# A fused linear-attention and gated-MLP kernel: 24 normalizations on ScalarE, 52 low parts on GpSimd, a new order of all steps

## The chip, the core and the metric

The kernel runs on one core of a Trainium2 chip. The core's engines work side by side, each through its own queue in order: TensorE (PE, with its weight loads as PEld), VectorE (DVE), ScalarE (ACT), GpSimd (POOL) and SyncE (SP), which here only issues DMAs. Semaphores tie the queues together. The metric is the device time of one execution in microseconds, as the median of several runs.

## What is computed

For 8 batches of 576 tokens, 8 heads of 64 (512 channels), float32 throughout:

```python
kv  = einsum('bhsd,bhse->bhde', k, v); out = einsum('bhsd,bhde->bhse', q, kv)
x   = out / sqrt(mean(out*out, -1) + 1e-6) * g_norm        # then heads side by side: [b, 576, 512]
h   = gelu_tanh(x @ w_in); u, v = h[..., :512], h[..., 512:]
v_n = (v - mean(v)) / sqrt(var(v) + 1e-6) * g_ln           # per token
v_s = einsum('ts,bsd->btd', w_sg, v_n) + b_sg[None, :, None]
y   = x + (u * v_s) @ w_out
```

## The kernel before

Every float32 operand of the large matrix products is split into a high part, rounded to the matmul type, and a low part, the rest; each product is then three matmuls (high·high, high·low, low·high). The split costs, per operand tile, one cast and one subtraction on another engine.

The whole program is one hand-recorded list of steps, `ORDER`, with one name per step: a letter for the kind, a digit for the batch, a number for the tile, and for some kinds a last letter that names the engine (v DVE, a ACT, p POOL). Each engine executes its own steps in the order in which they stand in that list, so the list alone sets every queue, SP's too. `HOMES` is a second list that says which buffer each new tile takes.

The kinds that matter here, with their lines: `k` loads of k and v (L405) and `q` loads (L431); `K` k^T v (pkv, L414); `o` attention output (pq, po, L439), `e` its squares (L451), `f` its scaling (L459 on ACT, L461 on DVE); `s` sums of squares (pss, L484) and `t` the reciprocal roots (L514 to L528); `x` scaling to x (L568), `X` and `Y` its high and low parts (L230, L584); `U` and `u` the product and gelu of u (pu L666, L671); `V` and `a` the product and gelu of v (pv L615, L620), four chunks of 128 tokens a batch and one leftover chunk for two batches; `b` the statistics of v (L625, L626), `p` its reciprocal deviation on POOL (L630, L631), `y` its normalization on DVE (L636), `z` and `w` its high part (L230) and low part (L653); `S` the product over tokens (pg, L680, L683), `g` its scale and bias (L688), `G` the gate u·v_s on POOL (L693); `H` and `J` the high and low part of a gate, `R` a difference of two gates (L721), `h` and `W` its high and low part (L230, L709 for both kinds of low part); `P` the output product (py, L741), `Q` and `Z` its addition to x (L754); `O` the store. `N` is a matmul on zeros ("warm") that only fills time at the start. The output product uses seven block products of sums and differences instead of eight blocks, so `P72` is the third product of batch 7.

In steady state the batches overlap: TensorE's queue mixes `U` and `V` of one batch with `S` of the one before and `P` of the one before that, so that each step's operands are made while TensorE does something else. One casting helper (L230) serves all high parts.

Of the kernel before, what the change touches and what calls it, by code (L numbers as in the profile page):

```python
# [835 lines left out]
```

## Time and profile before

| | us |
|---|---|
| timed runs: median (lowest to highest of 3) | 496.63 (494.15 to 496.92) |
| the profiled execution's own time | 491.86 |
| its span, first to last instruction | 490.1 |
| TensorE matmuls busy | 482.1 (98%) |
| DVE busy | 351.3 (72%) |
| ACT busy | 179.8 (37%) |
| POOL busy | 159.1 (32%) |

Shares are averages over the span. TensorE's busy share counts overlapped matmuls and says little alone; what counts is whether its queue ever waits, stretch by stretch. An idle engine that nobody waits for costs nothing.

### The profile page before, as it was taken

What the parts mean: (1) busy time and instruction counts of PE and PEld (TensorE: products, weight loads), DVE (VectorE), ACT (ScalarE), POOL (GpSimd) and SP (SyncE); (2) the same over time, 40 slices, a digit from 0 to 9 for tenths busy, and PEclk for the clock granted to TensorE, in tenths of its full rate; (3) what the DMA queues carried; (4) which work ended last, traced back from release to release, by engine and by line L of the source; (5) the groups of instructions that cost most, each with busy time, mean ns of one, the idle gap of its engine ahead of it and who ended that gap; (6) DMA issues with size and microseconds to landing.
All of it is one profiled execution on the core that took longest, in us unless ns stands there. A gap on an engine that the chain in (4) does not pass through costs nothing.

```text
span 490.1 us, 10060 instructions
## 1 busy us (share of the span) xinstructions
PE 482.1 (98%) x3989; PEld 440.8 (90%) x3989; DVE 351.3 (72%) x809; ACT 179.8 (37%) x442; POOL 159.1 (32%) x204
## 2 busy tenths in 40 slices
PE   6999999999999999999999999999999999999997
PEld 6668889998998999988998998998998899998997
DVE  1698698888777786468765875577767687577576
ACT  1668575155234331142223323335033332123220
POOL 0333142652232323332143113342305232442551
PEclk9999999999999999999999999999999999999999
DMA  8996793054343612064535443300331021100033
GB/s 228 361 353 232 220 277 104 2 157 141 104 142 89 142 43 74 1 192 130 175 75 185 117 104 117 100 1 1 97 104 49 1 62 43 49 1 0 2 122 120
DMA packets 33658, 55.36 MB, mean 113 GB/s; under 512 B 7308, under 2 KB 9228, under 8 KB 33612
## 3 DMA queue, kind: packets, MB, share of 16 engines
q1 hardware_dynamic: 33612, 54.73, 37.1%
q8 instruction: 31, 0.51, 0.4%
q14 instruction: 15, 0.12, 0.1%
HBM read 44.76 MB, written 9.95 MB: 112 GB/s over the span
## 4 chain that ended last, share of the span: by engine, by line
PE 96%; DMA 2%; DVE 0%; ACT 0%; SPq 0%; issue 0%
PE pu L666 21%; PE pg L680 21%; PE pv L615 20%; PE py L741 18%; PE pkv L414 5%; PE pg L683 3%; PE po L439 3%; PE pss L484 2%; DMA kv_first<-in_vx 1%; DMA kv_first<-in_kx 1%; PE psq L468 1%; PE pq L439 1%; PE pb L552 1%; PE warm L270 0%; SPq L405 0%
## 5 line engine op out<-in xcount | busy, mean ns | idle before, releaser
L693 POOL TENSOR_TENSOR u<-gt,u 128x288 f32<-128x288 f32 x64 | 56.3, 890 | 116.3 <-DVE gt L688 113.6
L680 PE MATMUL pg<-wsh,vh 128*128 128x288 f32 x256 | 75.8, 296 | 0.0
L680 PE MATMUL pg<-wso,vh 128*128 128x288 f32 x256 | 75.4, 294 | 0.0
L680 PE MATMUL pg<-wsh,vo 128*128 128x288 f32 x256 | 75.4, 294 | 0.0
L754 DVE SCALAR_TENSOR_TENSOR x<-py,x 128x288 f32<-128x288 f32 x112 | 49.4, 451 | 28.7 <-PE py L741 28.3
L709 DVE TENSOR_TENSOR g<-u,g 128x288 fp32r<-128x288 f32 x112 | 56.2, 517 | 15.7 <-ACT g L230 13.0
L688 DVE SCALAR_TENSOR_TENSOR gt<-pg,glt,b_bc 128x288 f32<-128x288 f32 x64 | 32.3, 512 | 35.2 <-PE pg L683 34.9
L741 PE MATMUL py<-g,woh 128*128 128x288 f32 x256 | 55.9, 295 | 0.0
L230 ACT CAST g<-u 128x288 fp32r<-128x288 f32 x75 | 30.8, 434 | 68.2 <-POOL u L693 52.3
L671 ACT ACTIVATE u<-pu 128x288 f32<-128x288 f32 x64 | 25.7, 411 | 68.3 <-PE pu L666 67.1
L680 PEld LDWEIGHTS pg<-wsh,vh 128*128 128x128 f32 x256 | 48.2, 188 | 0.8 <-DVE gt L688 0.4
L680 PEld LDWEIGHTS pg<-wso,vh 128*128 128x128 f32 x256 | 48.1, 188 | 0.1
L680 PEld LDWEIGHTS pg<-wsh,vo 128*128 128x128 f32 x256 | 48.1, 188 | 0.0
L666 PE MATMUL pu<-xh,wuh 128*128 128x288 f32 x256 | 45.5, 299 | 0.0
L721 POOL TENSOR_TENSOR u<-u 128x288 f32<-128x288 f32 x33 | 29.4, 894 | 49.6 <-DVE g L709 40.9
L666 PE MATMUL pu<-xo,wuh 128*128 128x288 f32 x256 | 44.3, 295 | 0.0
L666 PE MATMUL pu<-xh,wuo 128*128 128x288 f32 x256 | 44.3, 295 | 0.0
L620 ACT ACTIVATE hv<-pv 128x512 f32<-128x512 f32 x32 | 19.0, 598 | 66.5 <-PE pv L615 59.5
L741 PEld LDWEIGHTS py<-g,woh 128*128 128x128 f32 x256 | 42.7, 188 | 0.6 <-issue 0.4
L741 PE MATMUL py<-g,wxh 128*128 128x288 f32 x192 | 41.5, 295 | 0.0
L666 PEld LDWEIGHTS pu<-xh,wuh 128*128 128x128 f32 x256 | 37.6, 188 | 3.7 <-issue 1.9
L741 PE MATMUL py<-g,woo 128*128 128x288 f32 x128 | 37.8, 295 | 0.0
(123 smaller groups left out, 1005.6 us busy)
## 6 DMA issues: line engine op xcount, KB each, us to landing
q<-in_qT SPq DMA_DIRECT2D x32, 288.0 KB, 5.5
out_y<-x SPq DMA_DIRECT2D x28, 288.0 KB, 2.9
bc<-rd SPq DMA_DIRECT2D x28, 256.0 KB, 3.9
k<-in_kx SPq DMA_DIRECT2D x24, 256.0 KB, 4.9
v<-in_vx SPq DMA_DIRECT2D x24, 256.0 KB, 4.8
kv_first<-in_kx SPq DMA_DIRECT2D x8, 256.0 KB, 6.3
kv_first<-in_vx SPq DMA_DIRECT2D x8, 256.0 KB, 5.4
words<-in_wu SPq DMA_DIRECT2D x4, 512.0 KB, 8.4
```

What stands on the lines that cost most here:

```text
L230: e.copy(dst, src) if e is ac else e.tensor_copy(dst, src)
L414: nc.tensor.matmul(part["kv", b][64 * r : 64 * r + 64, n * 64 : n * 64 + 64], k_[b, c][:, h], v_[b, c][:, h], start=(c == 0 and n == 0), s ...
L615: nc.tensor.matmul(pv, a[cc], w[:, cc, :], start=(n == 0), stop=(n == 11))
L666: nc.tensor.matmul(pu[:, :HS], w[:, cc, f], a[b, cc][:, t], start=(i == 0), stop=(i == 11))
L671: ac.activation(u_[b, n], part["u", b, n][:, :HS], AF.Gelu_apprx_tanh, scale=W_UP)
L680: nc.tensor.matmul(ps[:, :HS], a[:, d], w[:, c, t], start=(i == 0), stop=False)
L688: ve.scalar_tensor_tensor(g_[b, n], ps[:, :HS], glt[:, dc : dc + 1], b_bc[:, half(n // 4)], op0=ALU.mult, op1=ALU.add)
L693: po.tensor_tensor(u_[b, n], g_[b, n], u_[b, n], op=ALU.mult)
L709: ve.tensor_tensor(lo, src, f32(hi), op=ALU.subtract)
L721: e.tensor_tensor(dst, x, y, op=ALU.subtract)
L741: nc.tensor.matmul(y_[b, bank][c][:, :HS], wo_block(h, blk, e)[:, block(c)], a, start=(start and i == 0), stop=(i == 5), skip_group_check= ...
L754: ve.scalar_tensor_tensor(xs, y_[b, bank][c][:, :HS], W_UP, xs, op0=ALU.mult, op1=ALU.add)
```

## The change

Three things change. (1) `y` gets an engine: 24 of the 36 normalizations go from one DVE instruction to three ACT instructions (negate the mean, multiply by the reciprocal deviation, then one activation with a scale and a bias per partition). (2) The low parts `J`, `W` and `w` get an engine: 16 of 48 `J`, 26 of 64 `W` and 10 of 36 `w` go from DVE to POOL, the others stay on DVE. (3) `ORDER` and `HOMES` are replaced throughout. With it a few dozen further steps change engine (for instance `H` on ACT 39 instead of 31, `R` on POOL 29 instead of 33, `x` on POOL 4 instead of 8, low parts of weights on POOL 4 instead of 1), and 71 `N` instead of 69 stand in the list. The number of all other TensorE steps is the same.

```diff
@@ HOMES and ORDER: every row differs; a few of ORDER's
-    k01 k02 k04 D21 F21 D23 D02 A02 E02 B02v L02 C02 F02v I02v k00 N899 N898 N897 N896 N895 N894 N893 N892 N891 N890
-    W64 y70 R66p h66v R62v h63a u74 V72 H63v a71 W63 Q60 b71 h65a W65 z70a w70 W66 a72 Z56 b72 p71 V73 y71 U75 a73 b73
-    z71a w71 p72 p73 u72 P63 U76 Z60 y72 P62 Q63 z72a y73 u76 h62v z73a H67v J67 J63 R67p u75 w72 w73 J66 S71 g71 G71
...
+    k02 D23 D22 k04 D21 F21 k01 D00 A00 k00 N899 N898 N897 N896 N895 N894 N893 N892 N891 N890 N889 N888 N887 N886 N885
...
+    z52v R42v V53 w50v Q40 P41 G47 k73 Z40 Q41 a53 o61 b53 e63 Z41 e61 h44v W44v e67 f67v e65 w52p R43p K71 c70v s60
+    t60 U53 t61 t62 f65a f63a h43a W43v p53 y53a z53a t63 t64 t65 t66 q72 w53v f61a t67 t68 R45v U52 u53 w51p S53 g53
...
+    R63p V70 h62a a70 b70 h60v W60v h61a V71 a71 b71 p70 y70v V72 a72 W61v R65v z70a u70 p71 J66v R64v w70v V73 U73
+    b72 p72 O57 y71v a73 b73 u74 h63a P63 U77 P60 y72v h64v H63a W64v p73 y73v z71a z72a z73a w72v W63v H67a w71v J67v
+    w73v Q60 h65v W65p W62v u77 S77 g77 Z63 Z60 J63v u73 S71 g71 G71 R67v H71v P62 S75 g75 Q63 Q62 O56 S70 G77 Z62
@@ -631,8 +633,14 @@
         po.tensor_tensor(rs, rs, mhalf, op=ALU.pow)
         st_[b, c] = st_[b, c], rs
 
-    def v_norm(b, c):
+    def v_norm(b, c, e):
         mv, rs = st_[b, c]
+        if e is ac:
+            shift = T([P, 1], F32, "nb")
+            ac.mul(shift, mv[:, 0:1], -1.0)
+            ac.mul(shift, shift, rs[:, 0:1])
+            ac.activation(hv_[b, c], hv_[b, c], AF.Identity, bias=shift[:, 0:1], scale=rs[:, 0:1])
+            return
         ve.tensor_scalar(hv_[b, c], hv_[b, c], mv[:, 0:1], rs[:, 0:1], op0=ALU.subtract, op1=ALU.mult)
 
     def v_high(b, c, e):
@@ -647,10 +655,10 @@
                 part["vl", r] = T([P, F], F32R, "vl%d" % r)
                 cast(e, part["vl", r][s], hv_[b, c][s])
 
-    def v_low(b, c):
+    def v_low(b, c, e):
         if c < NC:
             hi, lo = vn_[b, c]
-            ve.tensor_tensor(lo, hv_[b, c], f32(hi), op=ALU.subtract)
+            e.tensor_tensor(lo, hv_[b, c], f32(hi), op=ALU.subtract)
         else:
             for r in range(2):
                 s, o = last_rows(r)
@@ -704,15 +712,15 @@
         gs_[b, key] = [T([P, HS], F32R, "h", 28, nm="g") for _ in range(2)]
         cast(e, gs_[b, key][0], src)
 
-    def split_low(b, key, src):
+    def split_low(b, key, src, e):
         hi, lo = gs_[b, key]
-        ve.tensor_tensor(lo, src, f32(hi), op=ALU.subtract)
+        e.tensor_tensor(lo, src, f32(hi), op=ALU.subtract)
 
     def gate_high(b, n, e):
         split_high(b, operand(n), u_[b, n], e)
 
-    def gate_low(b, n):
-        split_low(b, operand(n), u_[b, n])
+    def gate_low(b, n, e):
+        split_low(b, operand(n), u_[b, n], e)
 
     def combine(b, n, e):
 
@@ -726,8 +734,8 @@
     def combined_high(b, n, e):
         split_high(b, combined(n), combined_tile(b, n), e)
 
-    def combined_low(b, n):
-        split_low(b, combined(n), combined_tile(b, n))
+    def combined_low(b, n, e):
+        split_low(b, combined(n), combined_tile(b, n), e)
 
     def y(b, n):
         blk, op, bank, start, _ = PRODUCTS[n]

```

What the list moves is shown at three places, one engine each.

**SP's queue at the start.** The first loads of k and v (kv_first, the leftover rows k and v), constants (gnt, glt, ext) and weight words. Before:

```order
L405 DMA kv_first_77<-in_kx 128x512
L405 DMA kv_first_78<-in_vx 128x512
L405 DMA kv_first_77<-in_kx 128x512
L405 DMA kv_first_78<-in_vx 128x512
L405 DMA k_92<-in_kl 64x512
L405 DMA v_93<-in_vl 64x512
L295 DMA gnt_65<-in_gn 128x1
L300 DMA glt_67<-in_gl 128x4
L287 DMA words_100<-in_wu 128x2x512
L405 DMA kv_first_77<-in_kx 128x512
L405 DMA kv_first_78<-in_vx 128x512
```

Now:

```order
L407 DMA kv_first_77<-in_kx 128x512
L407 DMA kv_first_78<-in_vx 128x512
L302 DMA glt_67<-in_gl 128x4
L300 DMA ext_91<-in_ex 64x512
L407 DMA k_93<-in_kl 64x512
L407 DMA v_94<-in_vl 64x512
L297 DMA gnt_65<-in_gn 128x1
L407 DMA kv_first_77<-in_kx 128x512
L407 DMA kv_first_78<-in_vx 128x512
L289 DMA words_102<-in_wu 128x2x512
L407 DMA kv_first_77<-in_kx 128x512
L407 DMA kv_first_78<-in_vx 128x512
```

The constant `ext` (64x512) and `glt` stand ahead of the second pair of kv_first; the third pair, which was issues 10 and 11, is now 11 and 12.

**ACT's queue at the last v of batch 5,** from its gelu (hv<-pv) to its high part (vh). `sq` and `x<-po` belong to the attention of batch 6, `g` are casts of gates. Before:

```order
L620 ACTIVATE hv_4481<-pv_4459 128x512
L230 CAST g_4483<-u_3977 128x288
L230 CAST g_4486<-u_3866 128x288
L451 ACTIVATE sq_4517<-po_4505 128x288
L451 ACTIVATE sq_4519<-po_4508 128x288
L459 ACTIVATE x_4327<-po_4508,g8_66 128x288
L451 ACTIVATE sq_4547<-po_4511 128x288
L451 ACTIVATE sq_4549<-po_4514 128x288
L459 ACTIVATE x_4415<-po_4505,g8_66 128x288
L230 CAST vh_4600<-hv_4417 128x512
L230 CAST vh_4600<-hv_4481 128x512
```

Now:

```order
L622 ACTIVATE hv_4593<-pv_4557 128x512
L453 ACTIVATE sq_4611<-po_4598 128x288
L453 ACTIVATE sq_4614<-po_4595 128x288
L453 ACTIVATE sq_4620<-po_4604 128x288
L453 ACTIVATE sq_4623<-po_4601 128x288
L461 ACTIVATE x_4191<-po_4601,g8_66 128x288
L461 ACTIVATE x_4372<-po_4598,g8_66 128x288
L232 CAST g_4683<-u_3680 128x288
L640 ACTIVATE nb_4690<-mv_4608 128x1
L641 ACTIVATE nb_4690<-nb_4690,rs_4687 128x1
L642 ACTIVATE hv_4593<-hv_4593,nb_4690,rs_4687 128x512
L232 CAST vh_4553<-hv_4593 128x512
```

Between the gelu and the cast there are now the three instructions of the normalization (nb, nb, hv); one cast of a gate (g) and the high part of an earlier v chunk (vh) left the stretch. In the new list TensorE's steps between that v (`V53`) and the first product that reads it (`S53`) are `P41`, `o61`, `K71`, `s60`, `U53` and `U52`.

**DVE's queue at the last v of batch 7,** from its statistics to the low part that the next product needs. Before:

```order
L626 BN_AGGR mv_5903<-st_5902 128x2
L653 TENSOR_TENSOR vo_5859<-hv_5846,vh_5858 128x512
L754 SCALAR_TENSOR_TENSOR x_4327<-py_5713,x_4327 128x288
L636 TENSOR_SCALAR hv_5863<-hv_5863,mv_5867,rs_5908 128x512
L754 SCALAR_TENSOR_TENSOR x_4477<-py_5916,x_4477 128x288
L636 TENSOR_SCALAR hv_5900<-hv_5900,mv_5903,rs_5911 128x512
L230 CAST g_5964<-u_5353 128x288
L230 CAST g_5968<-u_5530 128x288
L709 TENSOR_TENSOR g_5969<-u_5530,g_5968 128x288
L709 TENSOR_TENSOR g_5844<-u_5304,g_5843 128x288
L653 TENSOR_TENSOR vo_5959<-hv_5863,vh_5958 128x512
L653 TENSOR_TENSOR vo_5959<-hv_5900,vh_5958 128x512
```

Now:

```order
L627 BN_STATS st_5920<-hv_5918 128x6
L628 BN_AGGR mv_5921<-st_5920 128x2
L644 TENSOR_SCALAR hv_5868<-hv_5868,mv_5910,rs_5913 128x512
L232 CAST g_5971<-u_5474 128x288
L717 TENSOR_TENSOR g_5972<-u_5474,g_5971 128x288
L644 TENSOR_SCALAR hv_5918<-hv_5918,mv_5921,rs_5978 128x512
L661 TENSOR_TENSOR vo_5984<-hv_5868,vh_5983 128x512
L717 TENSOR_TENSOR g_5927<-u_5433,g_5926 128x288
L661 TENSOR_TENSOR vo_5873<-hv_5845,vh_5872 128x512
L717 TENSOR_TENSOR g_5990<-u_5202,g_5989 128x288
L661 TENSOR_TENSOR vo_5984<-hv_5918,vh_5983 128x512
```

Two additions to x (x<-py) and one cast left the stretch, one low part (g<-u,g) joined it; the normalizations here stay on DVE. Between the last v and the first pg TensorE has four steps before (`U`, `P`, `U`, `P`) and four now (`U73`, `P63`, `U77`, `P60`).

## Rows read from the trace of the kernel before

**Rows 1.** The page's head: span, and busy time (share of the span) and instructions of TensorE's matmuls and weight loads, DVE, ACT and POOL.

```profile
span 490.1 us, 10060 instructions
PE 482.1 (98%) x3989; PEld 440.8 (90%) x3989; DVE 351.3 (72%) x809; ACT 179.8 (37%) x442; POOL 159.1 (32%) x204
```

**Rows 2.** Busy time by stretch: from:to in us, its length, then busy us (instructions) of PE, PEld, DVE, ACT and POOL, the granted TensorE clock, the mean busy share of the DMA engines, GB/s.

```profile
0.00:12.38 12.38, 8.31 (x46) 8.12 (x47) 1.67 (x11) 2.15 (x3) 0.19 (x4) 1.00 0.84 228
12.38:34.50 22.12, 21.45 (x263) 13.91 (x263) 17.49 (x40) 13.64 (x33) 6.81 (x6) 1.00 1.04 355
...
38.80:90.00 51.20, 51.20 (x373) 46.64 (x372) 43.39 (x98) 34.44 (x83) 17.03 (x22) 1.00 0.61 185
...
390.00:486.90 96.90, 96.85 (x687) 94.10 (x685) 70.17 (x159) 24.32 (x59) 37.47 (x45) 1.00 0.14 47
486.90:490.10 3.20, 0.00 (x0) 0.00 (x0) 0.45 (x1) 0.00 (x0) 0.00 (x0) 0.81 0.33 116
```

**Rows 3.** The chain of waits at the start, in order of time: start us, us, what.

```profile
6.80 5.46 DMA kv_first<-in_vx
...
12.39 2.87 PE pkv L414 x80
15.26 1.50 PE warm L270 x11
...
33.42 1.20 PE po L439 x16
...
37.54 1.34 PE pss L484 x31
38.88 6.57 PE pu L666 x48
...
51.98 1.23 PE pkv L414 x32
```

**Rows 4.** Groups of matmuls by line: operation, tiles, shapes, count, busy us, mean ns of one, and idle us of the engine before them.

```profile
L680 PE MATMUL pg<-wsh,vo 128*128 128x288 f32 x256 | 75.4, 294 | 0.0
L666 PE MATMUL pu<-xh,wuo 128*128 128x288 f32 x256 | 44.3, 295 | 0.0
```

**Rows 5.** The same view for the instructions that the change moves and their neighbours, on DVE, POOL and ACT.

```profile
L636 DVE TENSOR_SCALAR hv<-hv,mv,rs 128x512 f32<-128x512 f32 x32 | 18.4, 582 | 1.9 <-POOL rs L631 1.8
L653 DVE TENSOR_TENSOR vo<-hv,vh 128x512 fp32r<-128x512 f32 x32 | 22.0, 698 | 5.0 <-ACT vh L230 4.9
L709 DVE TENSOR_TENSOR g<-u,g 128x288 fp32r<-128x288 f32 x112 | 56.2, 517 | 15.7 <-ACT g L230 13.0 <-PE py L741 1.9
L754 DVE SCALAR_TENSOR_TENSOR x<-py,x 128x288 f32<-128x288 f32 x112 | 49.4, 451 | 28.7 <-PE py L741 28.3
L230 DVE CAST g<-u 128x288 fp32r<-128x288 f32 x37 | 12.5, 352 | 2.6 <-POOL u L721 1.8 <-POOL u L693 0.7
L721 POOL TENSOR_TENSOR u<-u 128x288 f32<-128x288 f32 x33 | 29.4, 894 | 49.6 <-DVE g L709 40.9 <-DVE u L721 8.2
L568 POOL TENSOR_TENSOR x<-x,bc 128x512 f32<-128x512 f32 x8 | 11.9, 1494 | 17.1 <-DMA bc<-rd 6.4 <-ACT xlh L595 5.3 <-DVE xlo L600 5.3
L631 POOL TENSOR_TENSOR rs<-rs,mhalf 128x1 f32<-128x1 f32 x36 | 23.0, 640 | 3.0
L620 ACT ACTIVATE hv<-pv 128x512 f32<-128x512 f32 x32 | 19.0, 598 | 66.5 <-PE pv L615 59.5 <-issue 5.5 <-DVE vo L653 1.5
L451 ACT ACTIVATE sq<-po 128x288 f32<-128x288 f32 x56 | 20.7, 414 | 16.3 <-PE po L439 15.7 <-PE py L741 0.3
L459 ACT ACTIVATE x<-po,g 128x288 f32<-128x288 f32 x41 | 20.1, 505 | 3.1 <-DMA out_y<-x 3.0
L230 ACT CAST vh<-hv 128x512 fp32r<-128x512 f32 x25 | 15.3, 621 | 6.9 <-DVE hv L636 6.9
L230 ACT CAST g<-u 128x288 fp32r<-128x288 f32 x75 | 30.8, 434 | 68.2 <-POOL u L693 52.3 <-POOL u L721 9.9 <-DVE u L721 3.9
L260 ACT ACTIVATE g<-eps 128x1 f32<-128x1 f32 x1 | 0.2, 202 | 0.0
L671 ACT ACT_TABLE_LOAD x1 | 1.3, 1283 | 0.0
```

**Rows 6.** Timeline of batch 7 between its last v and the first pg: start us, us, engine, line, operation, count.

```profile
448.00 0.69 PE L666 MATMUL pu<-xh,wuh 128*128 128x288 f32 x4
...
448.83 0.69 DVE L625 BATCH_NORM_STATS2 st<-hv 128x6 f32<-128x512 f32 x1 [1.40 <-ACT hv L620]
...
453.27 1.90 DVE L653 TENSOR_TENSOR vo<-hv,vh 128x512 fp32r<-128x512 f32 x2
...
453.43 1.19 POOL L721 TENSOR_TENSOR u<-u 128x288 f32<-128x288 f32 x1 [2.25 <-DVE g L709]
...
455.43 0.29 PE L680 MATMUL pg<-wsh,vo 128*128 128x288 f32 x1
```

**Rows 7.** Timeline of SP's DMA issues at the start: start us, us of the issue, what.

```profile
5.40 0.47 SPq L405 DMA_DIRECT2D kv_first<-in_kx  x1
6.80 0.33 SPq L405 DMA_DIRECT2D kv_first<-in_vx  x1
...
15.90 0.47 SPq L298 DMA_DIRECT2D ext<-in_ex  x1
```

**Rows 8.** The chain of waits in the middle: two blocks of 12 matmuls, the first right behind a block of small pkv matmuls.

```profile
109.92 1.79 PE pu L666 x12
...
113.31 1.59 PE pu L666 x12
```

More of the change, by code (lines that the diff above doesn't have):

```diff
@@ L166 @@
-    f60a a52 b52 p52 R44v R41v z50a z51a g43 G43 H43a h41v R46v y52 Z40 J43 W41 U55 V53 w51 G47 R43p Q40 O36 f64a u55
-    a53 h43a h42a P41 Q41 Z41 o61 e61 e63 f63a R45v b53 W43 K71 w50 c70v e65 e67 s60 t60 t61 p53 y53 t62 t63 h46v f61a
-    t64 H46v U54 z52a U56 z53a t65 t66 t67 w52 f65a t68 r60 u54 P43 W42 R47p w53 J46 h45v W45 Q43 u56 S50 g50 W46 r62
-    f67a S55 g55 G55 S56 g56 S54 h44a W44 Z43 G50 H47v J47 x61p P42 Q42 r61 x60v P45 Q45 U53 l63 U57 u57 g54 Z42 G54
-    H50a l61 q72 S51 l60 Z45 U52 X61a u53 P44 J50 Q44 h47a Y61v l62 r63 x62v S52 Z44 m6 X62a S53 n63 G56 O45 u52 x63v
@@ new lines @@
+    s13 t10 t11 t12 t13 t14 C06 t15 u02 F04a F05a U06 K20 t16 t17 I05v t18 U04 f16a D20 F20a F06a n03 I06v D16 D07
+    F16a I21v f17a A07 E07 D08 f11a B07a L07 C07 k23 A08 f15a D09 U05 u05 I20v A09 B09v r10 I04v F07a B08a I07v k24
+    D10 A10 n00 B10a u06 n01 n02 U07 K21 D14 V02 a02 A14 B14a E09 V01 L09 E08 D18 F18a u04 L08 E10 r12 x10v c20a L10
+    C08 F08v x11v r11 l12 l11 V00 a01 l13 l10 k30 b01 V03 m1 n10 I18v C10 b02 n11 X11a Y11v n12 n13 V04 k31 F10a X10a
+    a00 b00 E14 r13 p02 k32 x12v x13v y02a C09 L14 Y10v p00 K30 u07 X12a p01 X13a Y13v q31 Y12v V10 y00a C14 a04 b04
@@ new lines @@
+    D12 A12 z00a I10v y01a D15 D11 A11 F14v z01a w00v q21 B12v I16v p04 y04a D17 E12 L12 C12 I08v I14v B11v U15 u15
+    U11 u11 a03 b03 p03 F17a I17v U14 u14 z02a w02v d00v A15 z04a B15v D13 A13 D19 F19a F30v d01v a10 y03a U16 U12
+    I30v d02v E15 E13 k33 B13v L13 z03a w01v w03v u16 C13 V11 w04v I19v F32a V13 a13 k40 E11 L11 D24 q20 S02 g02 G02
+    F31a S06 a11 b11 d03v F33a p11 I31v S01 I32v S03 L15 H02v C15 F15a g01 G01 b10 S07 k34 I15v F09a I09v y11a b13
+    d04p F34a S05 C11 u12 p10 g07 d05v J02v G07 S04 H01a I33v g05 g03 G03 y10a F35a S00 d06v g06 z10a z11a G05 U10
@@ new lines @@
+    I34p g00 u10 J01v K31 k42 q22 g04 G00 H00a J00v p13 F11a R01v o20 P00 Q00 R03v H03a w10v G04 R00v I11v d07p h01a
+    e22 W01v e26 f26a c30a J03v I35v H07v f22a q30 V12 Z00 P01 Q01 Z01 h00a W00v U13 G06 R04p F36a P03 R05v y13a e20
+    f20a e24 f24v F37a I37p a12 U17 b12 p12 h05a h04a u13 H06a k41 q23 J06p w11p W05v I36v u17 y12a o21 W04v P02 J07v
+    e27 z12a z13a w13p Q03 Z03 P05 Q02 Q05 w12v e23 e21 e25 s20 t20 t21 f23a t22 t23 t24 t25 t26 t27 S12 t28 r20 f27a
+    r22 S17 g17 r21 R06v h06a R02v h02v W02v f25a h03a S11 g11 S10 Z02 W03p P04 Z05 R07p h07a g10 W07p G10 G11 H11a
@@ new lines @@
+    W06v g12 Z04 S14 Q04 g14 P06 G14 Z06 Q06 G12 f21v x20v S13 x21v g13 O05 H12a H10v J11v l21 S16 l20 X21a q32 J10v
+    S15 X20a g15 Y21v P10 l23 l22 m2 o30 e34 e32 Y20v f32a r23 K40 x22v x23v k51 g16 G16 X22a Y22v X23a e36 O06 G15
+    f34a Y23v V20 a20 O04 q33 e30 R11p R10p V22 a22 b22 U20 u20 f30a b20 U21 u21 k44 G17 k43 G13 O07 f36v o31 e31 e33
+    R13v n22 K41 e35 e37 s30 f37v t30 U26 J12v t31 t32 t33 h11a t34 t35 h10a f33a U24 n23 t36 t37 t38 R12p W10p R14v
+    q43 p22 y22v u26 U27 U22 u24 h12v W12p f31a V21 H16a h14a W14v u22 k50 J16v h13a c40a W11v a21 U23 n21 u23 q52
@@ new lines @@
+    f43a S34 g34 G34 Q26 r42 x41v x40v S37 r41 l42 O27 l43 l40 X40a S31 g31 G31 l41 m4 S35 g35 S32 S36 X41a g37 o50
+    e54 e50 f50a e56 G37 g32 Y41v G32 H32a S33 O25 n40 Q21 f54a r43 k64 x42v Y40v g36 G36 x43v g33 S30 K61 X42v Y42v
+    q53 o51 O26 f56a H37a H36a H31a J31p X43a Y43v e57 U45 c60v U42 g30 e52 G30 H30a J30v G35 U40 R31v f57a U44 e55
+    u45 R30p O24 e51 e53 q61 f52a P30 Q30 n42 J32v f53a s50 t50 t51 u44 U47 Z30 t52 U41 t53 t54 q62 t55 t56 J36p h31v
+    k71 t57 n41 R32p t58 k72 G33 u47 f51a u41 h30a W30v V40 J37v H33a a40 R34v u40 b40 U43 R36p h36a W31p P33 h34v
@@ new lines @@
+    q70 G51 u56 S54 g54 Q42 l60 l63 G50 l61 u52 r63 l62 X60a X61v Q43 S57 Z43 g57 J47p S55 g55 Z42 P45 Z45 W42p P44
+    S52 x62v Y61p Q44 Q45 O44 H51a Z44 G55 P46 x63v X63a Y60v H50a o70 e72 e76 O45 X62v Y62p Y63v e74 f74a J50p g52
+    G52 G56 Q46 U61 m6 J51v n62 f76a G57 H57a G54 V60 e70 R50p R52v h50v V63 V62 O46 f70a a60 H52a a63 b63 R51v Z46
+    h51a W51p R53v a62 o71 e75 e73 e71 W50p R54p H53a J57p e77 f77v U67 b60 b62 s70 u67 H56a f75a n60 t70 t71 t72 h52a
+    R55p t73 t74 t75 t76 W52v t77 h53a p62 h54a W54v t78 U62 P53 Q53 Z53 p60 O47 f72a u61 f73a u62 P50 Z50 y60a Q50
@@ L187 @@
+    W75p R72v h74a W74p Q73 h72a g72 Z70 Z73 U72 W72v u72 P61 Q61 Z61 O65 H77a J76v J77v P72 O66 P75 O67 Z72 Q72 Z75
+    Q75 O75 O74 P74 G72 H72a J72p R76p Z74 Q74 h76a O64 R77p O76 h77a P71 Q71 O77 Z71 W76p O70 W77p P76 Q76 O71 O72
+    Z76 O73
 """.split()
```

119 lines of the change are left out of this document (45 added, 74 removed), and 30 rows, old and new, of tables (h, ps).

## The prediction, made before the changed kernel ran

> **What bounds the kernel now.** I read the page's head first: matmuls are busy for 482.1 of 490.1 us, DVE, ACT and POOL much less [rows 1]. Since that share counts overlapped matmuls, I looked next at the windows, stretch by stretch. From 38.8 us to the last matmul at 486.9 us TensorE is busy throughout at a granted clock of 1.00 (its 2.4 GHz level), and only 3.2 us follow [rows 2]. The groups of matmuls agree: large ones of pg and pu have no idle time before any matmul [rows 4]. So behind 38.8 us no other engine's work ends late, and nothing taken off DVE, ACT or POOL there can make the kernel faster: it can only be made slower, by a wait that is not there today.
>
> That leaves the first 38.8 us. The chain of waits shows what they hold: DMA until 12.26 us (the value half of the third pair of k and v, issued at 6.80), then the short serial attention of batch 0 with warm matmuls as filling, and from 38.88 the dense stream [rows 3].
>
> The profiled execution took 491.86 us, its span and 1.8 around it. The median of the timed runs is 4.8 us above that; its three runs lie 2.8 apart. I make the sum against 491.86 and carry the 4.8 over.
>
> **The change, part by part.**
>
> *Normalizations.* 24 DVE instructions of 582 ns go: 14.0 us less on DVE. On ACT each is three. The small ones: 202 ns for a 128x1 activation with a constant scale. A per-partition scale is dearer, as the scaled copy of the attention output against its square shows, 505 to 414 ns at one size, so 91 per such operand, and 0.29 us for the second small one [rows 5]. The large one is not in the trace; from below it is the cast of that shape, 621 ns, from above that cast with two such operands, 803. I take 0.80, since it carries both. Together 1.29 us (1.11 to 1.29), 31 us more on ACT, whose 179.8 of 490 us have room.
>
> *Low parts.* 42 of 128x288 leave DVE at 517 ns and 10 of 128x512 at 698: 28.7 us less. On POOL the nearest rows are its subtraction at 128x288, 894 ns, and its product at 128x512, 1494 ns [rows 5]: 37.5 + 14.9 = 52 us more. The smaller moves (four differences and four scalings back to DVE, about 6 us; three weight parts to POOL, eight casts to ACT) nearly cancel there. DVE comes to about 351 - 14 - 29 + 4 = 312 us, ACT to about 215, POOL to about 205. None is near TensorE, so all this costs nothing as long as each operand still comes in time.
>
> *Does it?* Two places, chosen because there the slack is smallest or the new work is on the chain.
>
> At the end of batch 7 DVE begins the last statistics at 448.83 and ends the two last low parts at 455.17, where 6.34 us have gone; TensorE reads them at 455.43, 0.26 us later [rows 6]. In the new queue that stretch lacks two additions (0.90) and a cast (0.35) and has one more low part (0.52): 0.73 us shorter. The four TensorE steps that cover it are four again. So the tightest wait gets looser, to about 1 us.
>
> At the last v of batch 5 the new chain is on ACT. TensorE's cover is `P41` (1.6 us), `o61` (1.2), `K71` (16 of pkv, half of 1.23), `s60` (1.34), `U53` (1.8) and `U52` (1.6) [rows 3, 8]: 8.1 us to the first pg, and nine matmuls (1.2) more to the fourth chunk, which is the one that waits. ACT needs 0.6 for the gelu, then must wait for the attention output (up to 3 us after the v), then four squares (1.66), two scalings (1.01), a cast (0.43), the normalization (1.29) and the high part (0.62): 8.0 us, with the cover at 9.3. The low part on DVE adds 0.7, against a deadline two matmuls later, 9.6. The slack is some 0.9 us, and 1.1 if the large activation costs its lower bound. The statistics (0.69) and POOL's power (0.64) run beside the squares [rows 5, 6]. Late by more than that, TensorE waits; I take zero.
>
> *Locks.* DVE and POOL hold each other up. The two low parts at 453.27 took 1.90 us, where two of them are 1.40 by the mean, and a POOL subtraction next to them took 1.19 instead of 0.89 [rows 5, 6]. With 52 more POOL instructions this happens more often; DVE has some 40 us fewer to be hit. The lower end is nothing lost at TensorE, the upper end is in the rivals. The Trainium skill speaks against this part of the change: its page "SBUF — State Buffer", section "SBUF: two separate sides", says that DVE instructions with two SBUF inputs and GpSimd share one pair of ports, an exclusive lock for a whole instruction. Taken at its worst, 52 us of added POOL time would hold DVE for as long, so that DVE would be back at about 364 us; the rows above agree that the two block each other, and no row shows that TensorE paid for it.
>
> *Queue positions at the start.* On SP the 64x512 constant now stands ahead of the pair that ends the first wait. Its issue takes 0.47 us [rows 7]; its 131 kB at the 228 GB/s of that stretch take 0.57 [rows 2]. Bounds 0 (the queue already pauses for 0.9 us ahead of the issue at 6.80) and 2 us (a whole extra slot); I take 0.5. Three more warm matmuls ahead of it lie inside TensorE's wait. Behind it there are 22 warm matmuls instead of 23, at 1.50/11 each [rows 3]: -0.14. ACT's table load for the gelu (1.28 us [rows 5]) now stands ahead of the copy of batch 1's k^T v. In the worst case it delays that copy and the first u by its whole length; but the copy waits for 80 small matmuls first (2.87 us at their first use [rows 3]), and with the load only five casts stand in that gap, so zero.
>
> *Breaks in the stream.* Blocks of small matmuls between the large ones cost 0.2 us at the return, 1.79 against 1.59 for 12 [rows 8]. TensorE's new order has 22 such breaks for 20: +0.4.
>
> *End.* The last product, addition and store are the same steps: 0.
>
> Sum: 491.86 + 0.5 - 0.1 + 0.4 = 492.7 in a profiled execution, and with the 4.8 that the median stood above it, **497.4 us**, no change that this kernel's measurement could tell: I take 1% (5 us) as the least that it can.
>
> **Rivals.**
>
> *Late low parts (slower).* Locks and ACT's longer chain make the last v of each batch late at its first pg. It decides where the delay passes the 0.9 to 1 us worked out above; one locked instruction (0.3 to 0.5 us) and one POOL instruction more in front (0.9) would do. If the operand is delayed by 1.8 us in seven batches, TensorE waits 7 x 0.85 = 6 us: 503.4. For it: 0.26 us of slack today, and 0.9 at the new place. Against: DVE is freer by 40 us, and in the trace not one such delay reached TensorE. Chance 0.20, mostly above 1%. What the Trainium skill's page says of the lock would come out as this rival.
>
> *The 4.8 us come back (faster).* If the timed runs lie above the profiled one because small delays eat slack like those 0.26 us, a list with longer covers wins them back: 497.4 - 4.8 = 492.6, still within 1%. To pass 1% the start would have to shrink as well, of which only the warm matmuls (3.1 us) are free. For it: the runs' 2.8 us of scatter. Against: the profiled execution shows no such wait at all. Chance 0.17, of which 0.09 passes 1%.
>
> *The start slips (no change).* The constant or the table load costs its upper bound: 497.4 + 1.5 = 498.9. Chance 0.10. That the change does not do what it says is not a case of its own: the queues show the moves.
>
> The forecast itself keeps 0.53. Faster by over 1%: 0.09; slower by over 1%: 0.19; within: 0.72. The range runs from 492, just under the second rival, to 503.5, the first rival's time; about 0.1 lies above and 0.08 below.
>
> **What would show it.** In the profile after: DVE near 312, ACT near 215, POOL near 205 us; three ACT rows for the normalization that add to 1.1 to 1.3 us; the first pkv between 12.4 and 13.1; no idle time before pg, pu, pv and py behind about 39 us; at the last v of batch 5 an ACT chain that ends about 1 us ahead of its reader. Wrong would be: waits of pg or py on an ACT, POOL or DVE row that add to over 1 us, a first dense block later than 41 us, or a profiled execution below 490 us, which would say that I have missed time that could be saved.

## The result and the profile after

The changed kernel takes 501.08 us (median of 4 runs, 500.75 to 502.30), the kernel before 495.39 (4 runs, 493.41 to 496.92): a ratio of 1.0142 with a 95% interval of 1.011 to 1.0173. It is 1.4% slower. The time lies inside the range (492 to 503.5), but the forecast was no change, within 1%. The profiled execution of the changed kernel took 500.77 us, so this time the median stands 0.3 above it, not 4.8. Medians and ratios here leave out one slow execution, of 518.49 us in experiment 5.

The page's head answers to [rows 1]:

```profile
span 499.0 us, 10159 instructions
PE 486.0 (97%) x3991; PEld 443.4 (89%) x3991; DVE 315.0 (63%) x735; ACT 211.1 (42%) x517; POOL 201.5 (40%) x251
```

The engines' loads came out as computed (312, 215 and 205 were forecast). The windows show where the time went; they answer to [rows 2], with the same columns:

```profile
12.38:34.50 22.12, 21.06 (x231) 14.06 (x232) 15.28 (x33) 12.21 (x31) 7.67 (x6) 0.92 0.99 328
34.50:38.80 4.30, 3.15 (x45) 2.40 (x43) 3.13 (x8) 4.29 (x12) 0.00 (x0) 1.00 0.91 272
38.80:90.00 51.20, 49.63 (x416) 43.32 (x416) 38.50 (x93) 37.24 (x88) 18.29 (x20) 0.97 0.75 226
90.00:190.00 100.00, 98.78 (x846) 90.19 (x846) 66.44 (x162) 48.14 (x124) 43.53 (x58) 1.00 0.32 99
190.00:290.00 100.00, 100.00 (x887) 92.94 (x884) 59.04 (x134) 34.97 (x89) 38.49 (x48) 1.00 0.36 107
290.00:390.00 100.00, 100.00 (x776) 91.26 (x774) 59.47 (x138) 39.01 (x94) 44.36 (x53) 1.00 0.24 70
390.00:495.50 105.50, 105.20 (x760) 101.28 (x760) 71.32 (x161) 33.18 (x80) 49.01 (x64) 1.00 0.13 43
```

From 190 us on TensorE is idle for 0.3 us in 305.5, though most of the moved work stands there. The losses are ahead of 90 us, plus 1.2 us between 90 and 190, and the granted clock, 1.00 in every stretch of [rows 2] that has matmuls, is 0.92 and 0.97 in two. TensorE's waits by what ended them (total us, times, longest us), without one for the first matmul on zeros that both kernels have:

```profile
PE pkv L416 <- DMA kv_first<-in_vx: 3.3, 1, 3.3
...
PE pkv L416 <- DMA v<-in_vl: 1.4, 1, 1.4
PE po L441 <- DVE x L463: 1.2, 1, 1.2
PE po L441 <- ACT kvf L232: 1.2, 1, 1.2
PE py L749 <- DVE g L717: 0.3, 1, 0.3
```

The chain of waits ties those on kv_first, on v's leftover rows (v<-in_vl) and on kvf, the copy of batch 1's k^T v, to their places (compare [rows 3]):

```profile
6.58 6.57 DMA kv_first<-in_vx
...
13.29 4.24 PE pkv L416 x80
...
34.00 1.25 ACT L265
...
36.00 0.28 ACT kvf L232
...
45.37 1.16 PE pss L486 x32
...
51.05 0.50 SPq L407
...
51.59 5.36 DMA v<-in_vl
...
57.09 0.68 PE pkv L416 x16
57.77 8.38 PE pv L617 x29
```

The third pair of k and v lands 0.9 us later than before. The load of the gelu table (34.00) stands shortly ahead of the copy of kvf on ACT, with an activation and the cast of a weight between. And v's leftover rows for batch 2 are issued only at 51.59: on SP they stand behind the store of batch 1's reciprocal roots (L541), which ends at 50.94, because the sums of squares (pss) that begin that chain come at 45.37 instead of 37.54. What the clock did behind the first wait (on kv_first) and behind the one on the leftover rows:

```profile
13.00:14.00 1.00, 0.71 (x14) 0.74 (x16) 0.69 (x1) 0.00 (x0) 0.23 (x1) 0.66 0.98 296
14.00:16.00 2.00, 2.00 (x43) 2.00 (x42) 0.00 (x0) 0.00 (x0) 1.06 (x1) 0.50 1.01 375
16.00:18.00 2.00, 2.00 (x39) 1.87 (x36) 0.42 (x2) 1.23 (x2) 0.00 (x0) 0.82 1.08 409
...
56.00:58.00 2.00, 0.91 (x17) 0.87 (x18) 1.89 (x6) 1.31 (x4) 0.00 (x0) 0.92 1.07 293
58.00:60.00 2.00, 2.00 (x5) 1.52 (x5) 1.26 (x4) 0.73 (x3) 0.74 (x1) 0.50 1.08 209
60.00:62.00 2.00, 2.00 (x8) 1.63 (x7) 0.00 (x0) 0.00 (x0) 0.00 (x0) 0.72 1.02 262
```

Behind both it is at 0.50, the 1.2 GHz level: the 80 pkv matmuls take 4.24 us where they took 2.87, and 29 of pv take 8.38 where they would take 6.7 at the pace of 12 of them in the chain of the kernel before, which ran at 1.00:

```profile
323.03 2.77 PE pv L615 x12
```

By these rows the two falls cost 1.4 + 1.7 = 3.1 us. What the granted clock lacks in the six windows (0.34 + 1.00 + 0.36 + 0.16 + 1.00 + 0.56) is 3.4 us, an estimate from above.

The account, against the profile before: first wait 1.0 (3.31 for 2.29), kvf 0.7 (1.15 for 0.47), leftover rows 1.6 (1.43 and 0.14 in two pieces), clock 3.4, po near 159 us 1.2, end 0.6 (0.3 for py, and 0.3 more behind the last matmul): 8.5 of the 8.9 us by which the span grew, or 8.2 with the clock at 3.1. It sets one execution against one. Between the medians lie 5.7 us: the profile before is of one of the shortest executions, as the part on the 4.8 us shows.

### The profile page after: what moved, and what is told of

Read it like the earlier page. It is cut to its first block, busy times and chain, and to the rows that moved or that the text cites. A ratio compares the mean times of both kernels' runs of the same rounds, so it can differ in the third digit from the quotient of the medians.

```text
span 499.0 us, 10159 instructions
## 1 busy us (share of the span) xinstructions
PE 486.0 (97%) x3991; PEld 443.4 (89%) x3991; DVE 315.0 (63%) x735; ACT 211.1 (42%) x517; POOL 201.5 (40%) x251
## 4 chain that ended last, share of the span: by engine, by line
PE 90%; DMA 4%; DVE 2%; ACT 1%; SPq 1%; issue 1%; DVEq 0%; ACTq 0%
PE pg L688 21%; PE pv L617 20%; PE pu L674 19%; PE py L749 18%; PE pkv L416 4%; PE pg L691 3%; PE po L441 3%; DMA kv_first<-in_vx 2%; PE pss L486 2%; DMA out_y<-x 1%; DMA v<-in_vl 1%; PE psq L470 1%; SPq L407 1%; PE warm L272 0%; DVE g L717 0%
## 5 line engine op out<-in xcount | busy, mean ns | idle before, releaser
L701 POOL TENSOR_TENSOR u<-gt,u 128x288 f32<-128x288 f32 x64 | 57.3, 906 | 81.9 <-DVE gt L696 67.9
L762 DVE SCALAR_TENSOR_TENSOR x<-py,x 128x288 f32<-128x288 f32 x112 | 48.2, 450 | 30.0 <-PE py L749 29.5
L232 ACT CAST g<-u 128x288 fp32r<-128x288 f32 x80 | 33.4, 433 | 67.7 <-POOL u L701 28.9
L717 POOL TENSOR_TENSOR g<-u,g 128x288 fp32r<-128x288 f32 x42 | 35.4, 849 | 53.8 <-ACT g L232 26.9
L717 DVE TENSOR_TENSOR g<-u,g 128x288 fp32r<-128x288 f32 x70 | 35.1, 513 | 12.5 <-ACT g L232 12.0
L627 DVE BATCH_NORM_STATS2 st<-hv 128x6 f32<-128x512 f32 x32 | 22.0, 688 | 31.9 <-ACT hv L622 31.8
```

The lines of the kernel that those rows point to most:

```text
L232: e.copy(dst, src) if e is ac else e.tensor_copy(dst, src)
L627: ve.bn_stats(st, hv_[b, c])
L701: po.tensor_tensor(u_[b, n], g_[b, n], u_[b, n], op=ALU.mult)
L762: ve.scalar_tensor_tensor(xs, y_[b, bank][c][:, :HS], W_UP, xs, op0=ALU.mult, op1=ALU.add)
```

## The experiments

**Theory 1:** the new list's start (waits on loads, one table load, and the clock that falls behind them) and one store cost the time; the moved normalizations and low parts cost TensorE nothing. **Rival:** the moved work is late. Line numbers in these kernels can be one lower than in the changed kernel.

**1. A shorter first wait.**

```diff
     N861 N860 N859 N858 N857 N856 N855 N854 N853 N852 N851
+    N700 N701 N702 N703 N704 N705 N706 N707 N708 N709 N710 N711 N712 N713
     K00 k03 B00v E00
```

> The changed kernel with 14 more matmuls on zeros in front of its first k^T v step; nothing else moves. Theory 1 (start and clock): the changed kernel lost its time in the first 62 us; there TensorE idles 3.3 us for the third pair of k and v, its granted clock then falls to the lower level (0.50 between 14 and 16 us), and the first 80 pkv matmuls take 4.24 us instead of 2.87. The added matmuls take 0.11 to 0.14 us each and cut the idle time to about 1.5 us; the pair lands at 13.1 us as before, the clock stays at 1.00, the block takes about 2.9 us, and the span falls from 499.0 to about 497.4 (median from 501.1 to about 499.5). Rival (the moved work is late): the start has nothing to do with it, the span stays at 499.0 within 0.3. Third (the clock falls for another reason than the idle time): the block still takes 4.2 us.

Measured: 499.77 us median, ratio to the kernel before 1.010 (1.0056 to 1.0145). The wait fell to 1.57 us, the pair landed as before and the clock stayed at 1.00 behind it, as theory 1 says. But the profiled span is 498.6, 0.4 less only: in this execution the clock fell later, where TensorE waited for nothing. Windows from 20 us on:

```profile
20.00:34.50 14.50, 14.35 (x104) 8.10 (x98) 12.35 (x28) 11.56 (x28) 5.96 (x5) 0.88 1.05 310
34.50:38.80 4.30, 3.83 (x58) 3.05 (x58) 1.32 (x4) 2.18 (x7) 0.00 (x0) 0.50 1.03 373
```

The other three executions have spans of 496.0, 497.4 and 499.1 us at mean clocks of 1.000, 0.996 and 0.993. So the clock can fall at a second place, and not in every execution. The execution at 1.000 shows the loss without the clock: 496.0 is 4.3 to 6.0 us above the seven executions of the kernel before at 0.999 or 1.000 (490.0 to 491.7 us), where the account without its clock term has 5.1.

**2. The gelu table behind the copy of kvf.**

```diff
-    E05 K10 K11 K12 K13 i C01 F01a Y00v I03p K14 c10a X04a
+    E05 K10 K11 K12 K13 C01 F01a Y00v I03p K14 c10a i X04a
```

> The changed kernel with the load of the gelu table moved behind the copy of batch 1's k^T v (kvf) on ACT. Theory 1: TensorE's wait of 1.35 us in front of the first po behind 35 us is this table load, 1.28 us on ACT ahead of the copy; the wait shrinks to 0.1 to 0.2 us, the first pu starts at about 36.3 instead of 37.5 us, and the span falls by 1.2 us to about 497.8. Rival a (ACT's other work there, four xlh copies and a cast of a weight, is what is late): the wait stays over 0.6 us. Rival b (the time is given back, because the wait for v's leftover rows at 55.4 us is set by a DMA and not by TensorE): first pu earlier, wait at 55.4 longer by as much, span unchanged.

Measured in one execution: the wait for kvf is 0.47 us instead of 1.15, but the span is 499.9, since here the first pkv started only at 14.26 us, behind a wait of 4.83. And the 0.47 is also there in three kernels with the table in its old place (experiments 1 and 4 and the half list with the new start), whose clock was at 0.50 in the pkv matmuls ahead; where these ran at full clock with the table ahead it was 1.14 to 1.15 (three profiles). The table load costs 0.7 us, and only when TensorE arrives early enough. The expected gain of 1.2 was too high.

**3. The leftover rows one product later.**

```diff
-    U07 K21 D14 V02 a02
+    U07 D14 V02 K21 a02
```

> The changed kernel with the second k^T v step of batch 2 (the leftover rows) one v product later on TensorE. Theory 1: its wait of 1.4 us for v's leftover rows, which stand on SP's queue behind the store of the reciprocal roots, goes, since the product of 12 matmuls (2.8 us) lies in front of it, and with it the fall of the clock to the lower level from 58 to 61 us that cost some 1.7 us more: the span falls by about 3.2 us to about 495.8. If the clock's fall is not caused by this wait: by 1.5 us alone, to 497.5. Rival (the v product is not ready either, its operands are late because of the moved work): the wait moves to pv and the span stays within 0.4 of 499.0.

Measured in one execution: span 496.3, 2.7 us less (the changed kernel's four spans lie 1.5 us apart). The wait is gone, no other came in its place before 90 us, and the clock is 1.00 from 38.8 to 90. So the v product was ready (against the rival), and the gain is near the 3.2 that theory 1 expected for the wait and the fall behind it, together the largest piece of the account. That the wait brings the fall with it is not shown. In the kernel of experiment 4 it is just as long and ends at 61.1 us, and the clock behind it stays at 1.00:

```profile
PE pkv L415 <- DMA v<-in_vl: 1.4, 1, 1.4
...
62.00:64.00 2.00, 2.00 (x10) 1.65 (x10) 1.26 (x5) 0.69 (x3) 0.74 (x1) 1.00 1.09 206
```

Nor does it fall behind the 1.28 us of this wait in the second kernel of experiment 5; behind 1.59 us in experiment 2 it does.

**4. Stores ahead of a load, and the end.**

```diff
-    K40 x22v x23v k51 g16 G16 X22a Y22v X23a e36 O06 G15 f34a Y23v V20 a20 O04 q33
+    K40 x22v x23v O06 O04 O07 k51 g16 G16 X22a Y22v X23a e36 G15 f34a Y23v V20 a20 q33
...
-    k43 G13 O07 f36v
+    k43 G13 f36v
...
-    H72a J72p R76p
+    H72a J72v R76p
...
-    Z71 W76p O70 W77p P76
+    Z71 W76v O70 W77v P76
```

> The changed kernel with two distant places put back: three stores of batch 0 stand ahead of the load of a k and v chunk of batch 5 on SP's queue (there they stood behind it, and it waits for a TensorE step), and the last three low parts go back from GpSimd to DVE. Theory 1: the wait of po at 159 to 160.5 us (1.2 to 1.6 us) is a buffer of x whose store landed late because it stood behind that load; it goes. The wait of 0.3 to 0.4 us of py at 489 us is DVE beside GpSimd at the very end; it goes. Span 499.0 less 1.6 to 2.0, about 497.2. Rival: the store is not what po waits for (ACT's or DVE's scaling is late by its own work): the wait stays, span 498.6 or more. If the tail holds only because of the order of DVE's steps: 497.4 to 497.6.

Measured in one execution: the wait of po is gone. The middle window of this kernel:

```profile
90.00:190.00 100.00, 100.00 (x847) 91.85 (x847) 67.81 (x164) 49.42 (x128) 44.10 (x59) 1.00 0.34 101
```

In the changed kernel the SP queue reached the third of these stores at 154.01 us, behind the loads k51, q33, k44 and k43; at k51 it had stood for 5.1 us until a TensorE step freed the buffer. The store landed at 159.9, and the scaling on DVE that needed its buffer held po. The second half failed: the wait of py at the end is 0.7 us, longer than with GpSimd (0.3). The span, 500.0, says nothing here: the clock was at 0.50 from 12 to 24 us and again near 36.

**5. The two halves of the change, each alone.** First the moved work in the old list (buffers of the kernel before), one row of it:

```diff
-    y73 u76 h62v z73a H67v J67 J63 R67p u75 w72 w73 J66 S71 g71
+    y73v u76 h62v z73a H67v J67v J63v R67p u75 w72v w73v J66v S71 g71
```

In the other rows 24 of 36 `y` get an a, and 52 of `J`, `W` and `w` a p, those that have them in the changed kernel.

> The moved work without the new order: the list of steps and the buffers of the kernel before, with the same 24 normalizations on ACT and the same 52 low parts on GpSimd as in the changed kernel. Theory 1 (the loss is the new list's start): the start is that of the kernel before, so nothing of the 1.4% comes back unless a moved step is late in a list that was not made for it: 494 to 497 us median, no clock of 0.5 in the first 62 us beyond what the kernel before shows, waits of pg and py at most 3 us together. Rival (the moved work itself costs: longer durations on GpSimd, three ACT instructions a normalization, the lock between DVE and GpSimd): slower by 4 us or more, 498 to 505, in waits of pg and py on GpSimd or ACT spread over the batches.

Then the new list with that work on DVE, again one row; all `y`, `J`, `W` and `w` get a v:

```diff
-    h43a W43v p53 y53a z53a
+    h43a W43v p53 y53v z53a
```

> The new order without the moved work: the changed kernel's list and buffers, with all normalizations and all these low parts on DVE again. Theory 1 (the start of the new list): the first 62 us hold hardly any moved step, so the loss stays: 499 to 502 us median, waits and clock falls of the start as in the changed kernel; behind 90 us DVE at some 0.85 of a hundred microseconds in the middle batches may add waits of its own, which would make it slower still. Rival (the moved work itself costs): it goes back to the time of the kernel before, 494 to 496.

Measured: 510.42 us (ratio 1.0328, 1.0294 to 1.0363) and 510.98 (1.035, 1.0286 to 1.0413). Both expectations of theory 1 fail: each half alone loses more than twice what the whole does. The first kernel shows what its rival named, waits of pg on GpSimd, with a time beyond the rival's range too; the rival of the second, a return to the time of the kernel before, fails as well. Some of TensorE's longest waits with the moved work in the old list, and then with the new list and all that work on DVE:

```profile
PE pg L687 <- POOL vo L660: 4.8, 3, 3.8
PE pv L616 <- ACT u L678: 3.8, 1, 3.8
PE pkv L415 <- DMA kv_first<-in_vx: 3.2, 1, 3.2
```

```profile
PE pv L616 <- DVE x L761: 2.5, 1, 2.5
PE py L748 <- DVE x L761: 2.2, 2, 1.3
...
PE pg L687 <- DVE vo L660: 1.2, 1, 1.2
```

So the moved work can stop TensorE, by up to 3.8 us at one low part, and in the new list (order and buffers) it does not. The waits of the second kernel's first 66 us are those of the changed kernel (3.42, 1.14 and 1.28 us), with nothing moved.

**6. All four places mended,** the moved work kept (edits 1 to 3 and the stores of 4).

> The changed kernel with all four places mended together: 14 more matmuls on zeros in front of the first k^T v step, the gelu table behind the copy of kvf, the leftover k^T v step of batch 2 one v product later, three stores of batch 0 ahead of a load; all moved work stays moved. Theory 1: the waits of 1.8 us (first pair), 1.2 (kvf), 1.4 to 1.6 (leftover rows) and 1.2 (store) go, and with them most of the time at the lower clock: median 494.5 to 496.5 against about 501.1, within 0.4% of the kernel before. Rival (moved work): 499 or more. If the clock falls in the first 40 us whatever TensorE waited for, as in the profile of the run with more matmuls on zeros, some 1.5 us stay: 496 to 498.

Measured: 496.96 us median of 12 runs (494.35 to 499.31), ratio 1.0058 (1.0035 to 1.0082) against 1.0142 for the change. Of the loss, 0.84% of 1.42% is gone, or about 4 us; the median is 0.5 above the range expected of theory 1, in that of the third case (496 to 498), and below the rival's 499. The profile is of one of its longest executions (499.16), yet all waits that the four edits aimed at are smaller or gone:

```profile
PE pkv L415 <- DMA kv_first<-in_vx: 2.1, 1, 2.1
...
PE pv L616 <- ACT wvh L231: 1.3, 1, 1.3
PE po L440 <- ACT kvf L231: 0.5, 1, 0.5
PE py L748 <- DVE g L716: 0.2, 1, 0.2
```

TensorE is at 100.00 of 100 us from 90 to 190, 190 to 290 and 290 to 390. A new wait of 1.3 us has come in front of pv: its weight's high part on ACT, which the old waits had covered. And the clock is at 0.50 from 30 to 40 us, as in experiment 1. The profiled span is 497.3, 3.5 us above the mean of the six executions at a mean clock of 0.999 or 1.000 (493.8). Ten of the other eleven have mean clocks of 0.996 and more and spans of 492.4 to 496.9; none of those was profiled, so what they still lose is not shown.

**7. Loads put off,** on top of 6.

```diff
-    k02 D23 D22 k04 D21 F21 k01 D00 A00 k00
+    k02 D23 k04 D21 F21 k01 k00
...
-    K00 k03 B00v
+    K00 k03 D22 D00 A00 B00v
```

> As the run with all four places mended, and the loads of ext (128 KB) and of the first weight (512 KB) moved behind the second pair of k and v on SP's queue, as the kernel before has ext. Theory 1: at the 380 GB/s that the stretch shows these 640 KB take 1.7 us, so the pair that TensorE waits for lands 1 to 1.7 us earlier, at 11.6 to 12.4 us; the weight that comes later (its steps were 20 us ahead of their use) costs nothing: 1 to 2 us below the other run, 493 to 495.5. Rival: the first weight's five steps on ACT, DVE and GpSimd are then late for the first pu, which waits as much longer: equal to the other run within 0.5.

Measured: 498.99 us (ratio 1.0115, 1.0073 to 1.0157), 2 us slower than 6. The first pkv does start 2.2 us earlier, at 11.34 us; then TensorE waits 0.7 us for the fourth pair, for q (now issued behind the loads put off), for the scaling ahead of the sums of squares, and 0.8 us for a later chunk of v:

```profile
PE pq L440 <- DMA q<-in_qT: 1.5, 1, 1.5
PE psq L469 <- DVE x L462: 1.0, 1, 1.0
```

The DMA engines' mean share from 5 to 34.5 us is 0.85 to 1.06, stretch by stretch, in the kernel before, the changed one, 6 and 7. I read this as little room in which a load that is put off could come in time; no run shows it apart.

**8. The lists cut and joined near 60 us.** The start of the kernel before with the rest of the change, and the reverse. Each pair of lines shows the steps around a seam, which lies at the line break:

```diff
+    A08 B08v E08 L08 V01 a01 f15a
+    i u03 u00 D10 A10 B10a u06 V02 a02
...
+    n00 B10a u06 n01 n02 U07 K21
+    u04 u07 D14 A14 E14 B14a
```

> A list put together from both: the first 250 steps of the kernel before (its loads, its matmuls on zeros, its first u products, up to about 60 us), then all other steps in the changed kernel's order, with all 24 normalizations on ACT and all 52 low parts on GpSimd. Buffers are dealt out anew to fit. Theory 1 (the loss is the start of the new list): the start looks like that of the kernel before, TensorE idle under 3.2 us before 66 us, no wait for v's leftover rows, and what is left behind it is the store's wait near 150 us (up to 1.2 us) and 0.2 us at the end: 494 to 496.5 us median, within 0.5% of the kernel before. Rival (the moved work costs, or the new order behind 60 us): 498 to 501.

> The other half: the first 244 steps of the changed kernel's list (up to the k^T v step that waits for v's leftover rows), then all other steps in the order of the kernel before, and nothing moved: all normalizations and all these low parts on DVE. Theory 1: the loss comes along without any moved work: the waits of 3 us (first pair), 1.2 (kvf) and 1.4 (leftover rows) and the clock at 0.50 near 14 and 58 us; 498.5 to 501 us median. Rival: 494 to 496. Waits behind 66 us that come from the seam of the two lists or from the dealt-out buffers are read off apart.

Measured: 504.59 us (ratio 1.0198, 1.0159 to 1.0237) and 510.05 (1.0315, 1.0268 to 1.0362). As totals both failed: behind 66 us TensorE has ten waits of 0.4 to 0.9 us in each, spread over the batches, where buffers had been dealt out anew. What can be read are the starts. Leaving out the wait for the first matmul on zeros, with the old start TensorE idles 3.36 us before 66 us and the clock stays at 1.00; with the new one, and nothing moved, it idles 6.81 us, waits 2.52 for the leftover rows, and the clock is at 0.50 near 14, 32 and 62 us. In the kernel before and in the changed one that idle time is 2.95 and 6.18. The start's loss needs no moved work.

A second try at the first joint kept each list's own buffers:

> Once more the start of the kernel before (268 steps, up to about 65 us) and behind it the changed kernel's order with all its moved work, this time with each list's own buffers on its side of the seam (none dealt out anew: in the first try at this, 13 waits of 0.4 to 0.9 us for buffers were spread from 120 to 460 us, and hid what was asked), and with the three stores of batch 0 ahead of the load of batch 5's chunk. Theory 1 (the moved work costs nothing behind the start, the whole loss is the new list's start, one store and 0.2 us at the end): TensorE waits under 0.8 us in all behind 66 us, span 490 to 492.5, median 493.5 to 496, within 0.4% of the kernel before. Rival (the moved work or the new order behind 65 us costs something that the start had covered): waits of pg, py or pu on GpSimd, ACT or DVE of 2 us and more together, median 497 or more.

Measured: 502.02 us (ratio 1.0167, 1.0142 to 1.0193). Missed again as a total: at the seam a pv product waits 4.4 us for a gelu on ACT (62.9 to 67.3 us), with the clock at 0.63 in the window from 66 to 70; and its first wait was 3.19 us, with a clock of 0.55 to 0.60 behind it. The ten waits are gone, and behind the seam it shows what it was made for:

```profile
90.00:190.00 100.00, 100.00 (x864) 91.94 (x864) 67.84 (x164) 49.46 (x128) 44.05 (x59) 1.00 0.33 99
190.00:290.00 100.00, 100.00 (x878) 92.89 (x875) 59.26 (x135) 34.94 (x89) 38.23 (x47) 1.00 0.37 107
290.00:390.00 100.00, 100.00 (x774) 91.04 (x773) 60.35 (x136) 38.86 (x95) 43.52 (x53) 1.00 0.23 70
390.00:490.00 100.00, 99.75 (x721) 95.99 (x722) 68.12 (x153) 32.66 (x79) 47.56 (x62) 1.00 0.10 32
```

That is 0.25 us of waiting in 400 with the moved work in place behind the seam and the three stores ahead of the load.

**9. The kernel before, with its own first wait filled.**

```diff
     N855 N854
+    N700 N701 N702 N703 N704 N705 N706 N707 N708 N709 N710 N711
     K00
```

> The kernel before with 12 more matmuls on zeros ahead of its first k^T v step, nothing else. It tells whether the kernel before pays for its own wait of 2.3 us there in executions that were not profiled (their mean granted clock is 0.993 to 0.997, that of the profiled one 0.999). If the clock falls in some of them for this wait: 0.5 to 1.5 us faster, 492.5 to 493.5 median, clocks at 0.998 or more. If the fall comes from elsewhere: equal within 0.3 us, clocks as before. If the added matmuls delay the first pair: up to 0.5 us slower.

Measured: 494.22 us, ratio 0.9996 (0.997 to 1.0021), mean clocks of 0.992 to 1.000 as in the kernel before. Filling its wait of 2.3 us down to 0.26 gained nothing: so a clock that falls behind this wait is not what the longer executions of the kernel before pay for.

## Why the prediction was right or wrong, point by point

**That nothing behind the start could be gained, and the moved work costs TensorE nothing: right, in the new list.** With all moves, and the stores put right, it waits 0.25 us from 90 to 490 (experiment 8). The sizes held:

```profile
L717 POOL TENSOR_TENSOR g<-u,g 128x288 fp32r<-128x288 f32 x42 | 35.4, 849 | 53.8 <-ACT g L232 26.9 <-DVE g L232 16.3 <-PE pkv L416 6.4
...
L642 ACT ACTIVATE hv<-hv,nb,rs 128x512 f32<-128x512 f32 x22 | 18.0, 817 | 0.7
...
L661 POOL TENSOR_TENSOR vo<-hv,vh 128x512 fp32r<-128x512 f32 x10 | 13.2, 1320 | 23.1 <-ACT vh L232 21.3 <-DVE vh L232 1.8
...
L641 ACT ACTIVATE nb<-nb,rs 128x1 f32<-128x1 f32 x24 | 7.1, 295 | 4.1 <-POOL rs L633 2.4
```

894, 800, 1494 and 290 ns were taken for these four.

**The last v of batch 5: right, with more slack than computed.** The timeline of its end:

```profile
349.69 0.20 ACT L640 ACTIVATE nb<-mv 128x1 f32<-128x1 f32 x1
...
350.31 0.82 ACT L642 ACTIVATE hv<-hv,nb,rs 128x512 f32<-128x512 f32 x1
...
351.15 0.62 ACT L232 CAST vh<-hv 128x512 fp32r<-128x512 f32 x1
...
352.52 0.68 DVE L661 TENSOR_TENSOR vo<-hv,vh 128x512 fp32r<-128x512 f32 x1
...
353.19 0.30 PE L688 MATMUL pg<-wsh,vh 128*128 128x288 f32 x1
```

The high part is there at 351.77 us; nine matmuls (1.2 us) into pg it is first read, near 354.4. That is 2.6 us of slack, where 9.3 - 8.0 = 1.3 was reckoned. The low part is there at 353.20 and read two matmuls later, near 354.7: 1.5 us, where 0.9 was reckoned.

**The locks: right that they cost TensorE nothing,** but at the very end one may: there DVE's last two low parts ran beside GpSimd and took 2.03 us (513 ns is the mean of one), py waited 0.3 us, and putting three back on DVE did not help. DVE's low part of 128x512 takes 770 ns in the mean instead of 698, that of 128x288 513 instead of 517 [rows 5]. The Trainium skill's page "SBUF — State Buffer", section "SBUF: two separate sides", has the exclusive lock; that the rows of 128x512 lengthen agrees with it, and those of 128x288 show nothing of it in the mean. Its worst case, DVE held for the whole of GpSimd's added time, did not come: DVE is busy 315.0 us, not 364.

**The start: wrong, and this is the step that failed.** "Queue positions at the start" priced three edits, found by looking at the heads of two queues, and summed them to 0.4 us. Of these the pair that ends the first wait was undersized: over eight profiles of lists with the new start (7 excepted) the first pkv stands at 12.6 to 14.3 us, mean 13.4, over five with the old one at 12.0 to 12.5, mean 12.3, so 1.1 us for the 0.5 taken, inside its bounds. The table load, "so zero", costs 0.7 where TensorE comes early. The cover of 80 small matmuls was there (32.48 to 35.1 us), and five casts were counted, but the work of ACT was not added up: from the arrival of x at 32.14 to the copy at 35.91 it has three further casts of x (1.10), four of x's leftover rows (0.69), the table (1.28), an activation of `eps` (0.20) and the cast of a weight (0.60, partly overlapped). The two largest waits had no term at all: the load of the leftover rows behind the store of the reciprocal roots (1.6 us) and the three stores behind a load (1.2). Both are SP queue positions, and SP's queue was read only up to 16 us.

**The clock: no term, and the largest item.** The sum priced each wait at its length. Behind two of them TensorE ran at 0.50, and the 3.1 to 3.4 us so lost are more than the 1.0 and 1.6 that these waits added. The profile before had 1.00 everywhere and so did not show that a wait can cost twice.

**The 4.8 us carried over: wrong, and it hid half of the error.** The sum for a profiled execution was 492.7 and came out at 500.8. Of 51 executions of the kernel before that ran beside the experiments, the seven at a mean clock of 0.999 or 1.000 have spans of 490.0 to 491.7 us, the six at 0.992 or less 492.7 to 495.9, and most lie at 0.995 to 0.997 with 491.0 to 493.7. Its profile (490.1 at 0.999) was from the fast end, and the clock is part of the difference that was carried: 1.3 us lie between the means of the first and the last of these groups (491.0 and 492.3). The changed kernel's four executions lie at 0.990 to 0.993 and 499.0 to 500.5, so nothing was to be carried over.

**The rivals.** *Late low parts* was the slower case and has the right sign and nearly the size (503.4), for the wrong reason: the changed kernel has no such wait but the 0.3 us of py at its end. It exists in experiment 5, where a low part on GpSimd stops TensorE for 3.8 us. *The start slips* named the right place, with 1.5 us for what came to some 7. *The 4.8 us come back* needed what no row showed. So it is luck that the time lies inside the range: its upper end was set by late low parts, which did not come, and the time was reached by waits and a clock that had no term.

**The signs.** The first pkv, 13.29 us, lies just outside the 12.4 to 13.1 named. Pg and py waited under 1 us in all, as forecast; the waits behind 39 us stood in front of pkv and po, which the list of signs left out.

**What stays open.** What the remaining 0.58% of experiment 6 is: at mean clocks of 0.999 and 1.000 its six executions have a mean span of 493.8 us, the seven of the kernel before 491.0, so some 2.8 us are not the clock. Its profile would account for them (an estimate, not tested): the first pkv 1.2 us later than before, 1.3 in front of pv, 0.5 at the end. Open too is what makes the clock fall behind one wait and not behind another as long, and why it fell between 30 and 40 us in five profiles (1, 4, 6, 7 and the reverse joint of 8) without a wait right ahead. No kernel with the moved work reached the time of the kernel before, so that the moves are free as a whole was shown by stretches, not by a total.
